# A fused sparse-attention and expert-attention kernel: the same 778 steps in another order, on other engines and buffers

## The chip, the cores and the metric

The kernel runs on one core of one Trainium2 chip. A core has five engines that run side by side, each with a queue of its own that it works off strictly in order: TensorE (PE, matmuls; its weight loads are shown apart as PEld), VectorE (DVE), ScalarE (ACT), GpSimd (POOL) and SyncE (SP, which here only issues transfers). POOL issues transfers too. PE writes to PSUM, a memory of 8 banks; DVE and ACT read it, POOL does not in this kernel. The metric is the time of one launch in microseconds (us), the median of several runs.

## What is computed

Two parts follow one another. The first is attention with 4 batches, 8 heads, 768 positions and 64 channels, in which a position sees its 31 nearest neighbours and 24 block summaries. The second sends the result x (4 x 768 x 512) through 4 causal attention experts, of which each position takes the best 2, weighted by a gate.

```python
k_sum = k.reshape(B, H, nb, 32, D).max(axis=3)
v_sum = v.reshape(B, H, nb, 32, D).mean(axis=3)
scores_l = scale * q @ k.T          # only where |i - j| < 16
scores_s = scale * q @ k_sum.T + log(32)
a = softmax(concat(scores_l, scores_s))
x = a @ concat(v, v_sum)            # heads side by side: (B, S, 512)
...
logits = x @ w_gate                 # top 2 of 4 experts, softmax over the two
for e in range(4):
    q, k, v = x @ wq[e], x @ wk[e], x @ wv[e]
    ye = causal_softmax(scale * q @ k.T) @ v @ wo[e]
    out += gate_weight[e] * ye
```

## The kernel before

**Tiling.** Stage 1 works on a pair of heads at a time (c = 0 to 3 in each batch b), stage 2 on a batch. The steps have names of a few letters followed by b, then c or another index. In stage 1:

- `dk`, `dq` (L285) load k and q through POOL's queue. In batch 0 the heads of pairs 2 and 3 come as one load (`dk010`, `dq010`), those of pair 1 and of pair 0 as one each (`dk001`, `dq001`, `dk000`, `dq000`). `dv` (L303 to L305) loads v through SP's queue into the tile vb, and `hc` (L181, shown as vb<-vb) copies the edge rows inside vb.
- `tk` and `tq` (L393) turn k and q on PE; `kw` and `cq` evict them from PSUM; `rk` (L410) takes the block maximum and `ksc` (kw<-ks) spreads it.
- `bs` (L322) sums blocks of v on PE, `be` (vs<-ps) evicts the sums and `ds` (vb<-vs) copies them into vb; for batches 2 and 3 POOL adds the blocks itself (`tr`, L367 and L370) and `ds` reads vu.
- `sc` (L435 and L441) are the scores, `ex` (L449) the exponential, `av` (L459) the product with v, `rc` and `xm` (L470, L474) the division, `tx` (L486) the turn of x, and `hi`, `lo` (L503) split x into two halves of half precision.

In stage 2: `vp` (L558, L561) makes v of all experts and the gate's logits, `v2` evicts the former, and `lg`, `ga`, `gx`, `gb`, `gc` (L568 to L607) turn the latter into gate weights. For two pairs of experts (cc = 0, 1), `pp` (L623) makes q and k, `pc` evicts them, `sp` (L647) are the scores in six units, `es` (L655) the exponential, `dm` (L660) the causal mask on POOL, `aw` (L671) the product with v, `r2` and `wv` (L691 to L698) the division and the gate weight, `tw` (L710) and `ct` turn the result; then `op` (L730) projects it, `oc` evicts it and `od` (L741) stores it. In the last batch the end is cut in two: `aw3?0` and `aw3?1` feed the cut of rows 0 to 511, `aw3?2` that of rows 512 to 767.

The weights of stage 2 come through POOL's queue: `dwq`, `dwk` (L516), `dwv` (L522, tile wvg) and `dwo` (L527). Small constants are set up once: `id16`, `id32`, `ke`, `mt`, `sel` on POOL, and clears (`vz`, `vone`, `kz`, `kwz`, `vtz`) on DVE or POOL. A few steps have a filler ahead of them (three matmuls on zeros, L169) that runs if the table gives it to PE and is left out if the table says N.

**What sets the order.** Nothing is scheduled at run time. `make_plan` lists 778 steps, each with the engines that may run it; `TABLE` is a list of entries `number,engine,slots`. `emit` goes through the table from front to back and writes each step's instructions to that engine's queue, with the buffer slots that the entry names. So the table's order, read for one engine, is that engine's queue, and a step waits for what it reads and for the last user of the slot that it writes. Some evictions and copies may run on two or three engines:

```python
R.step(f"hc{b}{c}", {"G": 1.65, "A": 1.45, "V": 0.9}, [vr[b, c]], [vb[b, c]], edge)
R.step(f"kw{b}{c}", {"V": 1.35, "A": 1.13}, [kp, kwpad], [kw], kwc)
```

The letters are V for DVE, A for ACT, G for POOL, S for SP and P for PE; the numbers beside them are not used in `emit`.

Of the kernel before, what the change touches and what calls it, by code (L numbers as in the profile page):

```python
# [58 lines left out]
101,P,3 102,A, 74,N,4 75,P,4 330,P,2.2.2 28,V, 76,A, 15,V, 80,P,0 81,P,1.1 97,N,4 45,N,3 79,A, 46,P,0 260,S,5 139,G,
333,V, 249,S,0 334,V, 33,N,6 82,P, 19,N,7 34,P,0 35,V, 332,A, 98,P,5 99,A, 428,G,0 50,A, 20,P,1 313,P,6.0.0 316,V,  # L60
314,P,2.2 318,A, 83,V, 84,V, 248,G,1 49,A, 51,N,4 52,P,0 21,V, 131,N,2 85,N,0 86,P,0.0 331,P,7.1 53,A, 315,A, 87,A,
132,P,1.1 22,V, 335,V, 88,V, 54,N,4 55,P,1 338,P,6.4 133,V, 32,A, 142,G, 427,G,2 57,N,0 58,P,1.2 36,V, 56,A, 59,P,
60,V, 261,G, 105,P,4.0.0 61,V, 103,N, 104,P, 134,V, 500,P,0.1.2 336,P,2.2 339,A, 141,G, 106,V, 337,A, 263,G, 107,V,
# [814 lines left out]
```

## Time and profile before

| | us |
|---|---|
| median of 3 runs (189.62, 191.22, 195.1) | 191.22 |
| the profiled execution: its time | 190.61 |
| the profiled execution: span from its first to its last instruction | 188.7 |
| PE busy in the span | 157.0 |
| chain that ended last: share of PE, DVE, ACT, DMA | 44%, 21%, 14%, 9% |
| packets of all DMA queues | 23.54 MB |

The profile gives the span of one execution, in which each instruction has a start and a length. What lies outside the span is 190.61 - 188.7 = 1.9 us. Of the rows that follow below, those of a timeline read: start, length, engine, line, operation, output tile <- input tiles, and in brackets how long the engine had been idle before and what released it. Those of a group read: busy time, mean length in ns, idle time before. Those of windows read: the stretch, its length, and the busy time of PE, PEld, DVE, ACT and POOL in it with the instructions in brackets, then the granted PE clock as a share of full speed, the DMA share, and GB/s.

### The profile page before, as it was taken

Reading aid. Unit: us, or ns where it says so; the run is one execution under the profiler, and the core shown is the slowest. Engines: PE = TensorE matmul, PEld = TensorE weight load, DVE = VectorE, ACT = ScalarE, POOL = GpSimd, SP = SyncE. Lnnn points to the kernel's source line nnn. Section 1 sums busy time; section 2 is a strip of 40 time slices with the busy share of each in tenths; the row PEclk is TensorE's granted clock in tenths of the full one; section 3 lists DMA queues with packets and bytes.
Section 4 is the critical chain, followed back from the end, with each engine's and each line's share of the span. In section 5 each row is a group of like instructions: output and inputs, shape, how many; then the busy total and the mean of one; then the engine's idle time right before and its main releaser. Section 6 shows DMA issues by size and latency. Waiting matters only on the chain.

```text
span 188.7 us, 7092 instructions
## 1 busy us (share of the span) xinstructions
PE 157.0 (83%) x3074; PEld 113.9 (60%) x3074; DVE 130.5 (69%) x253; ACT 121.2 (64%) x153; POOL 98.9 (52%) x155
## 2 busy tenths in 40 slices
PE   7419879598888997978899999897799998999670
PEld 2216668486666675865665688764575876547420
DVE  6794667899546789967629888696685684655740
ACT  2053376683568677868887886649688885697140
POOL 7868304983038269639847779129994141053000
PEclk9965589969999999999999999999999999999879
DMA  4999999999950006799969305498910530005325
GB/s 70 199 195 196 177 162 152 158 167 196 196 133 1 3 3 85 150 193 170 115 135 165 115 8 75 119 246 140 192 49 3 212 126 5 0 25 201 115 111 222
DMA packets 44207, 23.54 MB, mean 125 GB/s; under 512 B 33168, under 2 KB 39568, under 8 KB 44176
## 3 DMA queue, kind: packets, MB, share of 16 engines
q1 hardware_dynamic: 31136, 15.74, 40.6%
q0 software_dynamic: 13040, 7.34, 29.1%
q8 instruction: 24, 0.39, 0.9%
q14 instruction: 7, 0.06, 0.1%
HBM read 24.13 MB, written 6.29 MB: 161 GB/s over the span
## 4 chain that ended last, share of the span: by engine, by line
PE 44%; DVE 21%; ACT 14%; DMA 9%; issue 6%; POOL 3%; ACTq 1%; DVEq 0%; POOLq 0%
PE ps L623 9%; PE ps L459 8%; DMA wvg<-in_moe_wv_dram 5%; ACT a L655 5%; DMA qn<-in_q_dram 4%; PE ps L730 4%; PE ps L647 4%; PE ps L558 4%; ACT kw L179 3%; DVE vb L181 3%; DVE ks L410 3%; DVE x L474 3%; DVE lo L503 3%; PE ps L393 3%; PE ps L671 2%
## 5 line engine op out<-in xcount | busy, mean ns | idle before, releaser
L655 ACT ACTIVATE a<-ps 128x1024 f16<-128x1024 f32 (+1 forms) x48 | 42.1, 919 | 7.7 <-PE ps L647 6.0
L660 POOL TENSOR_SCALAR_AFFINE_SELECT a<-a 128x256 f16<-128x256 f16 x48 | 19.2, 418 | 39.0 <-ACT a L655 38.4
L449 ACT ACTIVATE aT<-ps 120x768 f32<-120x768 f32 x32 | 25.4, 814 | 14.1 <-PE ps L441 13.3
L459 PE MATMUL ps<-vb,aT 120*64 120x65 f32 x768 | 28.7, 231 | 1.6 <-issue 1.0
L459 PEld LDWEIGHTS ps<-vb,aT 120*64 120x64 f32 x768 | 26.1, 145 | 4.8 <-issue 3.3
L623 PE MATMUL ps<-hi,wqk 128*128 128x384 f16 x128 | 23.0, 327 | 1.4 <-DVE lo L503 0.5
L181 POOL COPY vb<-vb 32x1536 f32<-32x1536 f32 x11 | 16.4, 1501 | 8.0 <-DMA vb<-in_v_dram 7.6
L179 ACT COPY kw<-ps 128x1152 f16<-128x1152 f16 x13 | 14.4, 1118 | 9.5 <-DVE ks L410 9.0
L410 DVE TENSOR_REDUCE ks<-ps 128x24 f16<-128x768 f16 x16 | 15.2, 951 | 4.8 <-ACT kw L179 2.6
L647 PE MATMUL ps<-qk,qk 64*128 64x512 f16 (+3 forms) x128 | 15.7, 308 | 2.8 <-ACT a L655 1.5
L367 POOL TENSOR_TENSOR vt<-vt 120x1024 f32<-120x1024 f32 (+1 forms) x8 | 14.7, 1841 | 5.1 <-DMA vt<-in_v_dram 4.9
L623 PEld LDWEIGHTS <-wqk 128*128 128x128 f16 x128 | 12.0, 97 | 8.8 <-issue 1.1
L503 DVE TENSOR_TENSOR lo<-ps,hi 128x768 f16<-128x768 f32 x16 | 15.3, 954 | 1.7 <-ACT hi L179 1.5
L474 DVE TENSOR_TENSOR x<-ps,rec 128x768 f32<-128x768 f32 x16 | 15.3, 958 | 0.6
L558 PE MATMUL ps<-wvg,hi 128*128 128x264 f16 x96 | 14.0, 275 | 0.9 <-DVE ob L181 0.5
L671 PE MATMUL ps<-v,a 128*128 128x65 f16 x336 | 13.1, 194 | 1.9 <-DVE wav L698 0.8
L441 PE MATMUL ps<-qT,kw 64*128 64x64 f16 x384 | 12.1, 197 | 3.0 <-DVE qT L181 1.3
L730 PE MATMUL ps<-wo,wT 128*128 128x512 f16 x48 | 13.3, 406 | 1.5 <-ACT wT L179 1.1
L441 PEld LDWEIGHTS <-kw 64*128 64x128 f16 x384 | 10.7, 99 | 6.1 <-issue 2.9
L671 PEld LDWEIGHTS <-a 128*128 128x128 f16 x336 | 11.5, 97 | 4.3 <-issue 3.3
L179 ACT CAST qk<-ps 128x768 f16<-128x768 f32 x11 | 8.9, 806 | 6.5 <-PE ps L623 5.7
L322 PE MATMUL ps<-vb,sel 64*32 64x128 f32 x208 | 9.4, 307 | 4.3 <-POOL sel L266 3.5
(101 smaller groups left out, 289.3 us busy)
## 6 DMA issues: line engine op xcount, KB each, us to landing
vb<-in_v_dram SPq DMA_DIRECT2D x32, 176.0 KB
out_dram<-ob SPq DMA_DIRECT2D x11, 512.0 KB
vt<-in_v_dram SPq DMA_DIRECT2D x16, 192.0 KB
kn<-in_k_dram POOLq DMA_DIRECT2D x7, 384.0 KB, 6.5
qn<-in_q_dram POOLq DMA_DIRECT2D x7, 384.0 KB, 8.9
out_dram<-ob SPq DMA_DIRECT2D x2, 256.0 KB
vb<-in_v_dram SPq DMA_DIRECT2D x16, 24.0 KB
kn<-in_k_dram POOLq DMA_DIRECT2D x2, 192.0 KB, 8.6
```

The source lines that it names most:

```text
L179: nc.scalar.copy(dst, src)
L181: en(e).tensor_copy(dst, src)
L441: nc.tensor.matmul(s[:, hp, 64 * t:64 * t + 64], T["kw"][kw.slot][r, tt, :], T["qT"][qT.slot][r].rearrange("d (s p) -> d s p", s=8)[:, :, ...
L449: nc.scalar.activation(T["aT"][aT.slot][0:KR], pbank(sc, 2)[0:KR, :, 0:384], AF.Exp, scale=SCALE)
L459: nc.tensor.matmul(pbank(av, 2)[o:o + 64, u, 65 * (2 * (t // 2) + hp):65 * (2 * (t // 2) + hp) + 65], a[0:KR, hp, 64 * t:64 * t + 64], T[" ...
L474: nc.vector.tensor_tensor(T["x32"][x32.slot].rearrange("p (u t w) -> p u t w", u=2, w=64), avv()[:, :, :, 0:64], T["rec"][rec.slot].to_bro ...
L503: nc.vector.tensor_tensor(turned(T["lo"][lo.slot]), xpv(), turned(T["hi"][hi.slot]), AL.subtract)
L558: nc.tensor.matmul(p[:, i, 0:264], hi_(ch)[:, cols], T["wvg"][:, ch, :], start=(ch == 0), stop=False, skip_group_check=True)
L623: nc.tensor.matmul(pbank(pp, 2)[:, u, 0:384], T["wqk"][:, cc, ch, j, :], hi_(ch)[:, 384 * u:384 * u + 384], start=(ch == 0), stop=(ch == N ...
L647: nc.tensor.matmul(pbank(sp, 2)[:, ep, c0:c0 + w], T["qk"][qk[1].slot][r, 128 * tj:128 * tj + 128], T["qk"][qk[0].slot][r, n0:n0 + w], sta ...
L655: nc.scalar.activation(a2v(u), pbank(sp, 2)[:, :, 0:ln], AF.Exp, scale=SCALE / (XS * XS))
L671: nc.tensor.matmul(pbank(av, 2)[:, ep, 65 * ti:65 * ti + 65], a2v(u)[:, ep, o:o + 128], T["v2"][v2.slot][:, tj, 2 * cc + ep, :], start=(tj ...
```

## The change

Only `TABLE` changes; the steps, what they compute and the number of buffers stay.

```diff
 TABLE = """
-29,G,0 30,G,0 0,V, 112,P,0 66,P,1 91,P,2 114,P,3 5,G, 3,G,1 4,G,1 1,G, 123,N,4 89,N,6 16,V, 6,G, 258,G,2 11,V,
...
+29,G,0 135,S, 11,V, 0,V, 112,N,0 3,G,1 43,N,1 89,N,2 7,V, 66,N,3 9,V, 5,G, 8,V, 6,G, 14,G, 12,G, 90,P,0.0 93,V,
...
```

Every step is in both tables once. What differs is the order on each queue, the slots, and the engine of 83 steps. Of these:

| step | before | after |
|---|---|---|
| `kw` (16) | 3 DVE, 13 ACT | 7 DVE, 9 ACT |
| `cq` (16) | 8 DVE, 8 ACT | 12 DVE, 4 ACT |
| `ds` (16, two copies each) | 8 DVE, 8 POOL | 2 DVE, 12 POOL, 2 ACT |
| `hc` (16) | 1 DVE, 4 ACT, 11 POOL | 4 DVE, 6 ACT, 6 POOL |
| `hi` (16) | 8 DVE, 8 ACT | 6 DVE, 10 ACT |
| `pc` (16) | 5 DVE, 11 ACT | 7 DVE, 9 ACT |
| `ksc` (16) | 6 DVE, 6 ACT, 4 POOL | 4 DVE, 5 ACT, 7 POOL |
| `vone`, `vtz`, `v2o` (clears) | DVE | POOL |
| `cg` (gate weights to half) | POOL | DVE |
| fillers that run (3 matmuls each) | 6 | 2 |

**The start on POOL.** Before, POOL's queue begins with the loads of k and q for pairs 2 and 3 (kn_78, qn_74), and goes on to those of the other pairs (kn_79 and qn_75):

```order
L285 DMA kn_78<-in_k_dram 96x4x512
L285 DMA qn_74<-in_q_dram 96x4x512
L201 MEMSET id_64 128x128
L202 ISA
L202 AFFINE_SELECT id_64<-id_64 128x128
L285 DMA kn_79<-in_k_dram 96x2x512
L285 DMA qn_75<-in_q_dram 96x2x512
L285 DMA kn_79<-in_k_dram 96x2x512
```

After, the queue begins with the loads of kn_78 and kn_79 and the constants id16, ke, id32, vone and sel, of which the last row of sel stands first here; then come the q load, the masks, and a copy (`ksc03`) that reads a block maximum made by DVE, and the other loads behind that:

```order
L266 AFFINE_SELECT sel<-sel 64x4
L285 DMA qn_74<-in_q_dram 96x4x512
L224 MEMSET mt 128x128
L227 AFFINE_SELECT mt<-mt 64x96
L228 AFFINE_SELECT mt<-mt 64x96
L227 AFFINE_SELECT mt<-mt 64x96
L228 AFFINE_SELECT mt<-mt 64x96
L181 COPY kw_85<-ks_82 128x12x24
L285 DMA qn_75<-in_q_dram 96x2x512
L285 DMA kn_79<-in_k_dram 96x2x512
L285 DMA qn_75<-in_q_dram 96x2x512
L272 MEMSET vt_101 128x2112
```

The load of qn_74 moved from second place to behind 17 setup instructions, and those of pairs 1 and 0 to behind a wait for DVE; sel and vone moved ahead of all q loads.

**The end on DVE.** The gate weights of the last batch (gt_126) end with L607; what follows in DVE's queue before is the division of the last batch (cmb, wav) at once:

```order
L604 TENSOR_TENSOR ps<-gt_126,ps 128x24
L605 TENSOR_REDUCE gt_126<-ps 128x6
L606 RECIPROCAL gt_126<-gt_126 128x6
L607 TENSOR_TENSOR gt_126<-ps,gt_126 128x24
L691 RECIPROCAL ps<-ps 128x2x2
L693 TENSOR_TENSOR cmb_133<-ps,gt_126 128x2x2
L691 RECIPROCAL ps<-ps 128x2x2
L693 TENSOR_TENSOR cmb_132<-ps,gt_126 128x2x2
L698 TENSOR_TENSOR wav_135<-ps,cmb_133 128x2x2x64
L698 TENSOR_TENSOR wav_134<-ps,cmb_132 128x2x2x64
```

After, three evictions of the batch before stand between (wT, and ob of two outputs):

```order
L604 TENSOR_TENSOR ps<-gt_126,ps 128x24
L605 TENSOR_REDUCE gt_126<-ps 128x6
L606 RECIPROCAL gt_126<-gt_126 128x6
L607 TENSOR_TENSOR gt_126<-ps,gt_126 128x24
L181 COPY wT_137<-ps 128x2x6x64
L181 COPY ob_140<-ps 128x1024
L181 COPY ob_142<-ps 128x1024
L691 RECIPROCAL ps<-ps 128x2x4
L693 TENSOR_TENSOR cmb_132<-ps,gt_126 128x2x4
L698 TENSOR_TENSOR wav_135<-ps,cmb_132 128x2x4x64
```

The gate moved ahead of older work, and the larger cut (128x2x4) now comes before the smaller one (128x2x2).

**The end on ACT.** ACT evicts the last outputs (ob) and the last turned results (wT). Before:

```order
L179 CAST v_124<-ps 128x8x64
L593 ACTIVATE gt_126<-gt_126 128x24
L655 ACTIVATE a_131<-ps 128x256
L179 COPY ob_141<-ps 128x1024
L179 COPY wT_138<-ps 128x2x2x64
L179 COPY ob_140<-ps 128x512
L179 COPY ob_141<-ps 128x1024
L179 COPY ob_140<-ps 128x1024
```

After:

```order
L179 COPY ob_141<-ps 128x1024
L179 COPY wT_138<-ps 128x2x4x64
L655 ACTIVATE a_130<-ps 128x256
L179 COPY ob_140<-ps 128x1024
L179 COPY ob_142<-ps 128x1024
L179 COPY wT_138<-ps 128x2x2x64
L179 COPY ob_141<-ps 128x512
L179 COPY ob_140<-ps 128x512
```

The two outputs of 1024 columns now come ahead of the two of 512, and v and the gate's exponential have moved up out of this place. On PE the three `vp` of the last batch stand, before, behind 9 to 11 of its 12 `sp` and all its `pp`; after, behind 3 to 5 `sp` and ahead of the second pair's two `pp`.

More of the change, by code (lines that the diff above doesn't have):

```diff
@@ L59 @@
[L59 to L63, printed above, removed]
@@ L104 @@
-724,P,1.1.0 729,V, 762,V, 722,P, 730,V, 763,V, 755,P, 756,P, 758,V, 731,P,4.2 764,P,2.3 765,V, 596,S, 590,S, 759,V,
-723,P, 732,A, 772,P,2.0 773,A, 774,S, 725,V, 726,V, 760,P,6 727,P,4 761,V, 728,V, 775,P,3.2 776,V, 777,S, 766,P,0.1
-767,A, 768,S, 769,P,6.0 770,A, 771,S,
+29,G,0 135,S, 11,V, 0,V, 112,N,0 3,G,1 43,N,1 89,N,2 7,V, 66,N,3 9,V, 5,G, 8,V, 6,G, 14,G, 12,G, 90,P,0.0 93,V,
+113,P,1.1 39,P,4 116,A, 91,P,5 94,V, 13,G, 67,P,2.2 120,N,6 117,V, 70,V, 30,G,0 114,N,2 115,P,0 10,G, 25,N,0 71,V,
@@ new lines @@
+107,V, 21,V, 444,S,0 108,N,4 109,P,1.1 51,N,0 52,P,2 110,A, 333,V, 139,G, 136,G, 22,G, 140,G, 78,P,0 111,V, 18,V,
+57,N,2 28,A, 53,A, 292,N,4 293,P,1.2 297,V, 296,A, 445,G, 79,A, 80,N,0 81,P,0.2 58,P,1.0 82,P, 251,S,1 83,V, 84,V,
+446,G,0 59,P, 269,N,5 85,N,6 334,A, 338,P,0.1 60,V, 61,V, 314,P,4.0 318,V, 339,A, 62,N,2 63,P,2.2 142,V, 261,A,
+86,P,3.3 87,V, 264,N,4 88,V, 265,P,1 162,N,0 64,A, 65,V, 163,P,0 200,N,6 201,P,1 197,N,2 202,A, 266,V, 271,N,4
+164,V, 268,G, 207,N,6 249,S,2 270,P,2.1 274,V, 272,P,2 276,A, 198,P,2 143,N,0 144,P,0 16,G, 199,A, 219,N,2 220,P,0
@@ new lines @@
+472,P,0.2 473,A, 306,P,4.1.1 307,P, 432,G, 329,V, 308,V, 309,V, 288,N,6 232,N,0 233,P,0 234,A, 194,N,2 195,P,1
+196,V, 289,P,6.6 290,A, 310,P,4.7.7 311,A, 291,V, 429,S,5 430,A, 235,N,0 312,V, 236,P,0 237,V, 239,N,2 240,P,1
+612,S,2 389,P,6.2 500,P,4.1.0 390,V, 502,A, 610,S,4 484,P,5.2 488,V, 487,A, 503,V, 435,G,1 391,P,0.0 447,G, 437,G,
+491,P,6.0 392,V, 436,G, 449,P,5.2.2 452,V, 241,A, 501,P,4.0 402,P,0.0 451,V, 393,P,2 492,A, 347,P,6.1 394,A, 504,V,
+403,A, 353,P,2 354,V,5 350,P,0 355,V, 349,A, 505,A, 348,V, 352,A, 351,V, 356,V,1 597,G,2 357,A, 508,P,2.4 453,V,
@@ new lines @@
+611,G, 379,P,4 513,V, 374,A, 380,A, 370,P,6 461,V, 462,V, 623,G, 371,A, 398,G, 367,P,0 603,S,0 637,P,4.0 641,V,
+620,P,5.1 624,V, 463,P,2.2.2 368,A, 410,G, 395,G, 640,G, 644,P,6.0 645,A, 613,V, 627,P,4.5 628,A, 464,V, 465,V,
+401,G, 407,G, 413,P,0.0.0 514,P,6.3.3 625,P,4.3 412,P, 411,P, 515,A, 530,P,2.2 516,V, 604,G, 600,A, 531,A, 381,G,
+626,A, 414,V, 378,G, 605,G,1 375,G, 415,V, 532,P,6.0 372,G, 674,V, 678,P,2.4 607,G,0 533,V, 606,G, 238,S, 676,P,4.2
+601,S, 679,A, 642,P,0.1 677,A, 546,P,6.0 643,A, 630,P,2.1.0 654,P,4.1 658,V, 629,P, 631,V, 547,A, 534,P,0 535,A,
@@ new lines @@
+632,V, 416,P,4.2 417,V, 517,P,6.0 518,V,0 519,V, 523,P,2 525,V, 524,V, 537,P,4 538,A, 540,P,6 653,P,1.0.1 656,V,
+655,A, 520,P,2 522,A, 521,V, 526,V,0 559,P,4.1 366,G, 614,S,0 527,A, 528,V, 529,V, 369,G, 383,P,1.1.2 382,P, 541,A,
+560,A, 615,G, 616,G,0 539,G, 617,G, 384,P, 542,G, 549,P,0 550,A, 242,S, 657,G, 659,P,6.5 385,V, 386,V, 661,P,4.3
+660,A, 543,P,0 662,A, 387,P,2.3 388,V, 561,P,6.0 562,V, 618,A, 418,P,4.0 419,V, 544,A, 548,G, 421,P,2.1 422,A,
+420,S, 633,P,6.4.4 572,P,4.1 573,A, 563,P,0 564,A, 565,G, 634,V, 680,P,2.0.1 681,P, 575,P,4 566,P,0 635,V,
@@ new lines @@
+664,P,6.1.2 663,P, 576,A, 682,V, 683,V, 684,P,4.5.5 569,P,2 567,A, 568,G, 602,V, 646,P,0.0.0 647,P, 665,V, 666,V,
+685,A, 686,V, 424,P,6.0 648,V, 570,A, 649,V, 577,G, 571,G, 578,P,4 579,A, 425,V, 667,P,2.6.6 650,P,0.7.7 581,P,0.0.4
+574,G, 582,P, 580,G, 545,G, 583,P, 668,A, 669,V, 651,A, 733,P,6.2 536,G, 652,V, 735,P,2.0 736,A, 734,V, 551,G,
+554,P,1.1.0 552,P, 743,P,2.1 752,P,6 584,V, 585,V, 753,A, 426,S, 749,P,4 553,P, 687,P,6.1 555,V, 556,V, 750,A,
+688,V,0 744,A, 689,A, 690,P,4 692,A, 691,V, 751,G, 246,S, 557,P,2.0 737,P,6 423,S, 558,V, 746,P,4 747,A, 738,A,
@@ new lines @@
+693,P,2 694,V, 695,A, 696,V,1 697,A, 702,P,4.1 703,A, 740,P,6 700,P,2.0 741,A, 742,G, 586,P,4.1 739,G, 698,V, 699,V,
+701,A, 710,P,6.0 711,A, 712,G, 713,P,0 587,V, 748,G, 714,A, 715,G, 594,P,2.0 595,V, 707,P,6 708,A, 596,S, 745,G,
+588,P,4.2 589,V, 590,S, 709,G, 704,P,0 705,A, 706,G, 754,G, 716,P,2 717,A, 756,P,1.0.6 755,P, 591,P,4.1 718,G,
+592,A, 593,S, 722,P,0.1.0 758,V, 759,V, 723,P, 760,P,2.2 757,P, 761,A, 719,P,4 725,V, 726,V, 727,P,2.3 728,V,
+769,P,2.0 720,A, 770,A, 766,P,4.2 762,V, 771,S, 763,V, 721,G, 724,P, 764,P,2 729,V, 730,V, 767,A, 768,S, 731,P,6
@@ L107 @@
+732,V, 765,A, 775,P,0.1 776,A, 777,S, 772,P,1.0 773,A, 774,S,
 """
```

64 lines of the change are left out of this document (20 added, 44 removed).

## The prediction

> **What bounds the kernel now.** I read the busy line and the slices first, then windows of the stages, then the timeline of the two ends.
>
> ```profile
> span 188.7 us, 7092 instructions
> PE 157.0 (83%) x3074; PEld 113.9 (60%) x3074; DVE 130.5 (69%) x253; ACT 121.2 (64%) x153; POOL 98.9 (52%) x155
> ...
> DMA  4999999999950006799969305498910530005325
> ...
> 0.00:48.00 48.00, 34.40 (x725) 26.25 (x726) 36.62 (x70) 23.70 (x28) 28.34 (x54) 0.82 1.26 168
> 48.00:154.50 106.50, 96.67 (x2029) 72.20 (x2029) 76.95 (x140) 79.69 (x104) 65.45 (x88) 1.00 0.60 115
> 154.50:172.00 17.50, 16.77 (x202) 10.36 (x199) 10.05 (x16) 12.99 (x17) 4.68 (x12) 1.00 0.15 55
> 172.00:189.00 17.00, 9.21 (x126) 5.12 (x124) 6.92 (x27) 4.78 (x8) 0.41 (x1) 0.89 0.35 131
> ```
>
> PE is the busiest engine, but its waits lie unevenly. In the first window, up to the first `pp`, it is busy 34.40 of 48 us at a clock of 0.82, while the transfers run full (eleven slices of 4.7 us, to 52). In the middle it works 96.67 of 106.5 us at full clock: 9.8 us of waits. From 154.5 to 172 it hardly waits. In the last 17 us it is busy 9.21. So an order can win at most 10 us in the middle, and the rest at the two ends. I take each stretch by itself.
>
> **The start: -2.3 us.** The last `lo` of batch 0 on DVE releases the first `pp`:
>
> ```profile
> 47.99 2.76 PE L623 MATMUL ps<-hi,wqk 128*128 128x384 f16 x16 [0.51 <-DVE lo L503]
> ...
> 34.00:48.00 14.00, 10.31 (x255) 8.68 (x250) 13.50 (x22) 9.08 (x12) 9.49 (x13) 0.88 1.39 179
> ...
> L181 DVE COPY kw<-ps 128x1152 f16<-128x1152 f16 x3 | 3.9, 1333 | 0.0
> L181 DVE COPY qT<-ps 128x768 f16<-128x768 f16 x8 | 4.4, 552 | 0.2
> L181 DVE COPY vb<-vs 24x768 f32<-24x768 f32 x10 | 7.6, 797 | 0.1
> L181 DVE COPY vb<-vb 32x1536 f32<-32x1536 f32 x1 | 1.2, 1189 | 0.0
> L181 DVE COPY kw<-ks 128x288 f16<-128x288 f16 x6 | 1.7, 279 | 0.1
> L272 DVE MEMSET vt<- 128x2112 f32 x1 | 1.8, 1818 | 0.5 <-issue 0.5
> ...
> 174.68 0.18 DVE L607 TENSOR_TENSOR gt<-ps,gt 128x24 f32<-128x24 f32 x1
> ```
>
> DVE is full from 34 to 48 (13.50 of 14), so DVE's queue sets this end. Up to its last `lo` of batch 0 the new queue holds less: 3 `ds` of two copies, 6 x 0.80 = 4.8; 4 `ksc`, 1.1; `vtz`, 1.8. It holds more: 2 `kw`, 2.7; 2 `cq`, 1.1; 2 `hc`, 2.4; `cg`, four small operations like the one at 174.68, 0.7. That is 7.7 less and 6.9 more. The five small clears of `vone` leave too, at most 0.18 each; I count 0.6. If DVE idles as long as before, the first `pp` comes 1.4 us earlier. What is moved to POOL and ACT here lies under their own idle time (28.34 and 23.70 busy of 48).
>
> How long DVE idles is set by the loads and by PE's early speed:
>
> ```profile
> 3.79 0.15 PEld L169 LDWEIGHTS <-zz 128*128 128x128 f16 x1 [0.28 <-issue]
> 4.21 1.39 PEld L169 LDWEIGHTS <-zz 128*128 128x128 f16 x7 [0.27 <-issue]
> ...
> 7.72 0.90 PE L393 MATMUL ps<-ke,kn 100*64 100x100 f16 x32 [1.62 <-DMA kn<-in_k_dram]
> ...
> 14.51 1.91 PE L322 MATMUL ps<-vb,sel 64*32 64x128 f32 x26 [3.47 <-POOL sel L266]
> ...
> 17.11 0.88 PE L393 MATMUL ps<-ke,kn 100*64 100x100 f16 x16
> ...
> 22.89 2.40 PE L459 MATMUL ps<-vb,aT 120*64 120x65 f32 x48
> ...
> 1.35 0.82 POOL L285 DMA_DIRECT2D kn<-in_k_dram  x1 [0.85 <-POOLq L862]
> 2.17 0.68 POOL L285 DMA_DIRECT2D qn<-in_q_dram  x1
> ...
> 4.02 0.63 POOL L285 DMA_DIRECT2D qn<-in_q_dram  x1
> ...
> 11.15 0.22 POOL L224 MEMSET mt<- 128x128 f16 x1
> ...
> 12.41 0.26 POOL L228 TENSOR_SCALAR_AFFINE_SELECT mt<-mt 64x96 f16<-64x96 f16 x1
> ...
> DMA to landing us min/median/max: 4.8/8.9/13.9
> ```
>
> `bs03` waits 3.47 us for `sel` on POOL; `sel` now stands early, and this wait goes. In its place q is late. The five instructions of the masks run from 11.15 to 12.67, 0.30 each; 17 setup instructions are 5.2 by that. The q load, issued at 2.17 before, is issued at 1.35 + 0.82 + 0.65 + 5.2 = 8.0 after. The last row is the landing of the q loads, from the view of the tile qn: 12.8 at the least, 16.9 at the median. I take 13.5, near the least, because only two k loads stand ahead of it. From there PE has work without a gap: `tq03` and `tq02` 1.8, `bs01` and `bs03` 3.8, `sc030` 0.8, `tq01` 0.9, three `sc` 2.5, `tq00` and `tk00` 1.8, `av031` 1.2, `bs02` 1.9, `av030` 1.2, all at the speed of the rows at 14.51, 17.11 and 22.89 (an `sc` is an estimate, two of the shorter turns' pace): the end is at 29.4. Before, the same `av` ended at 25.3, without four of these steps (4.5). PE stands level.
>
> That was half speed. The spacing of the fillers' weight loads falls from 0.42 (3.79 to 4.21) to 0.20 (7 in 1.39): PE sped up after 3 us of unbroken work. Then it idled, and 16 turns at 17.11 cost what 32 did at 7.72. If the unbroken run from 13.5 lifts the speed likewise, `bs03` and `bs02` take half, 1.9 less, and DVE, which waits for both, gains up to 3.3 in all; if PE stays slow as it did before from 14.5 to 24, 1.4. I take the middle, **-2.3**. Of the six fillers four go; that costs at most two `tk` at half speed, 0.9, which lies under the wait for q. Ends: -4, and with late q (below) +4.6.
>
> [...]
>
> **The middle: +0.9 us.** From the first `pp` of batch 0 to that of batch 3 PE's work is the same but for steps that cross the edges: in come `tk12`, `tk23`, `sc130`, `sc121` and `aw210`, out go `bs12` and `tk11`. A `tk` is 0.45 (7.72), a `bs` 0.95 (half of 14.51), an `aw` of 12 matmuls 0.5 (175.30, below), and an `sc` 12.1 / 32 = 0.4 by the first row here:
>
> ```profile
> L441 PE MATMUL ps<-qT,kw 64*128 64x64 f16 x384 | 12.1, 197 | 3.0 <-DVE qT L181 1.3 <-ACT kw L179 0.9 <-issue 0.8
> ...
> 120.00:140.00 20.00, 16.74 (x320) 12.23 (x320) 16.04 (x33) 13.44 (x19) 13.55 (x15) 1.00 0.79 172
> 140.00:160.00 20.00, 19.47 (x382) 13.82 (x374) 12.69 (x18) 15.49 (x21) 7.20 (x14) 1.00 0.23 82
> ```
>
> The waits, 9.8, I leave. DVE's work there grows by some 5 us on 76.95, ACT's falls by some 7 on 79.69 (counted from the queues with the rows' lengths); both keep idle time. The waits' bounds are the worst and best window: 3.26 of 20 over 106.5 us would be 17.4 (+7.6), 0.53 of 20 would be 2.8 (-7.0). Two loads come later: `dwv` behind `ds00`, and `dwo` behind the last mask of batch 0's first expert pair. Their first users, `vp00` and `op00`, stand some 5 us and more of PE's work behind; I count 0.
>
> **The end: -2.8 us.** Before, `vp` ends late, and the gate on DVE (to 174.68) holds up the division:
>
> ```profile
> 175.30 0.53 PE L671 MATMUL ps<-v,a 128*128 128x65 f16 x12 [0.55 <-DVE cmb L693]
> 176.67 0.77 PE L671 MATMUL ps<-v,a 128*128 128x65 f16 x20 [0.84 <-DVE wav L698]
> 177.37 0.29 PE L710 MATMUL ps<-id,wav 64*128 64x64 f16 x8
> 177.60 0.41 PE L671 MATMUL ps<-v,a 128*128 128x65 f16 x8
> 177.81 0.28 DVE L181 COPY wT<-ps 128x256 f16<-128x256 f16 x1
> 179.00 0.40 PE L710 MATMUL ps<-id,wav 64*128 64x64 f16 x8
> 179.11 0.58 ACT L179 COPY ob<-ps 128x512 f32<-128x512 f32 x1 [1.09 <-PE ps L730]
> 179.72 5.04 SPq L741 DMA_DIRECT2D out_dram<-ob  x4
> 180.12 3.08 PE L730 MATMUL ps<-wo,wT 128*128 128x512 f16 x10
> ```
>
> After, `vp` stands ahead of two `pp` and seven `sp`, the gate hides under them, and the waits of 0.55 and 0.84 go: -1.4. Before, the last `aw` ends at 178.01 and the span 10.7 later. After, behind the last `aw` stand: division and gate weight 0.8 (estimated, five small operations), the turn 0.29, its eviction 0.28, two outputs of two matmuls (4 x 0.31 = 1.2 by 180.12), an eviction 0.58, six hand-overs of some 0.05, and the store; the last issue on SP ends at 184.76, the span 3.9 later. Sum 7.4: -3.3. Against that, more of PE's work stands ahead of the last `aw`: before, 0.8 of turns and 3.1 of outputs came behind it, after, 0.3 and 1.2; 2.4 more, less 0.5 of `aw210`: +1.9. Together **-2.8**. Ends: -4.8, if the smaller store lands in half the time, and -0.3, if ACT sets this end: its work from the last batch's first `pc` on is 2.5 us more than before.
>
> **Sum.** 188.7 - 2.3 + 0.9 - 2.8 = 184.5 of span; with 1.9 outside, 186.4, against 190.61 for the same execution. The median, 191.22, is 0.6 above that one, so I predict **187.0 us**.
>
> **Rivals.** Late q: `dq001`, `dk000` and `dq000` stand behind `ksc03`, which waits for `rk03` on DVE until about 11.5 (an estimate: three operations behind the first `tk`). Before, `dq001` was issued at 4.02; after, at 12. PE needs `tq01` at 19.9 in the walk above. At the longest landing, 13.9, it comes at 25.9: 6.0 late, and the speed-up is gone. The start is then -1.4 + 6.0 = +4.6, the span 191.4, the time **193.9**: slower than before. It decides from a landing of 11.2 us on. For it: the transfers run full. Against it: fewer loads stand in POOL's queue then.
>
> Given back: an order of three engines that each have 70 to 90% of work may wait more in the middle. At +4.2, some half of the way to the worst window, the time is 191.2, **no change**.
>
> Tighter: half of the way to the best window, -3.5, gives **183.5**.
>
> Slow end: ACT sets the end, and the start gains DVE's plain sum alone: -1.4 + 0.9 - 0.3, the time 190.4.
>
> **How the numbers follow.** A difference under 2% is about what a measurement of this kernel can't tell from none; the bounds are 187.4 and 195.0. The forecast has 0.42, with its own range 184.5 to 189.0, and 0.27 of it under 187.4; tighter 0.20, all faster; given back 0.16, of which 0.03 beyond 195.0; slow end 0.07, within; late q 0.15, of which 0.09 beyond 195.0, if the middle waits more too. Faster 0.47, same 0.41, slower 0.12. The range takes in all but the outer parts of tighter and late q: 182.0 to 194.5.
>
> **What would show it.** The first L623 at about 45.7 (the start is right from 44 to 46.6); the first L393 on qn at 13 to 14; PE's clock at 1.00 by 20 if the unbroken run lifts it; no wait of PE for `sel`; no wait of L671 for cmb or wav in the last 20 us; the last L671 some 7 us before the end. The forecast is wrong if the second group of L393 on qn comes after 22, if PE waits over 13 us between the two `pp`, or if ACT works without a gap in the last 15 us.

## The result and the profile after

| | before | after |
|---|---|---|
| median, us (5 runs each) | 191.22 | 188.52 |
| lowest to highest | 189.46 to 195.1 | 187.13 to 188.94 |
| the profiled execution: its time, its span | 190.61, 188.7 | 187.13, 185.4 |

The ratio is 0.9843, 95% interval [0.9801, 0.9885]: about 1.6% faster, which the bound of 2% calls the same. A second measurement (six runs, below as e13_after) gave medians of 189.67 and, before, 192.07, and a ratio of 0.9723 [0.9646, 0.98]. The ratios leave out the runs that lie over 1.5% above a kernel's fastest, and these kernels' runs scatter by about 3%, so that a ratio rests on a kernel's quicker runs (on two of the six in the second measurement) and can lie lower than the ratio of the medians.

These are lines of the page of the kernel after:

```profile
span 185.4 us, 7057 instructions
...
PE 152.6 (82%) x3062; PEld 112.2 (61%) x3062; DVE 132.5 (71%) x248; ACT 118.7 (64%) x148; POOL 100.0 (54%) x165
...
PEclk9996696996999969999999999999999999999996
DMA  4999999999599928669395689207200306300745
...
q8 instruction: 24, 0.39, 0.9%
```

The transfers run full up to the tenth slice, to some 46 us (before to the eleventh, 52 us), and again behind it from 51 to 65 us. PE is still the busiest engine. The windows that the prediction used, of the kernel after (columns as before):

```profile
0.00:48.00 48.00, 32.12 (x716) 25.85 (x718) 35.27 (x61) 20.86 (x25) 31.45 (x58) 0.86 1.31 165
48.00:154.50 106.50, 96.56 (x2042) 71.67 (x2035) 82.40 (x149) 78.62 (x98) 63.76 (x96) 0.98 0.56 102
...
34.00:48.00 14.00, 10.07 (x264) 8.86 (x257) 9.72 (x19) 8.53 (x11) 9.52 (x10) 0.88 1.54 163
```

In the first 48 us DVE is busy 35.27 us (36.62 before). From 34 to 48 us, where it had 0.5 us of idle time before, it is busy 9.72 of 14. Cut at the first `pp` (L623) of batch 0 and that of batch 3, the two executions compare thus:

| stretch, us | before | after | difference | forecast |
|---|---|---|---|---|
| start, to the first L623 of batch 0 | 47.99 | 48.32 | +0.3 | -2.3 |
| middle, to the first L623 of batch 3 | 106.5 | 106.3 | -0.2 | +0.9 |
| end, to the end of the span | 34.2 | 30.8 | -3.4 | -2.8 |

So in these two executions the whole gain lies in the end, and the start gave nothing. PE's timeline in the start of the kernel after, with its waits:

```profile
14.20 0.87 PE L393 MATMUL ps<-id,qn 96*64 96x96 f16 x32 [2.05 <-DMA qn<-in_q_dram]
14.99 3.49 PE L322 MATMUL ps<-vb,sel 64*32 64x128 f32 x52
...
19.17 0.85 PE L393 MATMUL ps<-id,qn 96*64 96x96 f16 x16
...
22.00 0.53 PE L393 MATMUL ps<-id,qn 96*64 96x96 f16 x16
...
26.51 0.55 PE L393 MATMUL ps<-ke,kn 100*64 100x100 f16 x16 [0.99 <-DMA kn<-in_k_dram]
26.89 0.51 PE L393 MATMUL ps<-id,qn 96*64 96x96 f16 x15
28.95 0.24 PE L393 MATMUL ps<-id,qn 96*64 96x96 f16 x1 [1.55 <-issue]
...
35.86 0.34 PE L435 MATMUL ps<-pi,mt 64*128 64x384 f16 x2 [0.92 <-issue]
...
37.80 0.55 PE L393 MATMUL ps<-ke,kn 100*64 100x100 f16 x16 [1.09 <-DVE lo L503]
...
41.78 2.31 PE L459 MATMUL ps<-vb,aT 120*64 120x65 f32 x48 [1.84 <-ACT aT L449]
...
48.32 1.93 PE L623 MATMUL ps<-hi,wqk 128*128 128x384 f16 x9
```

PE waits 6.4 us between 25.5 and 42 us: for a k load, for `lo` on DVE, for an exponential on ACT, and 2.47 us for "issue", which is nothing that the profile shows. (The kernel before has 4.8 us of waits from 25 us to its first L623.) The stall at 28.95 is odd: fifteen turns of q run, and the sixteenth, with the same operands at hand, comes 1.55 us late. DVE in turn waits for PE; this is its queue:

```profile
42.91 0.23 DVE L470 RECIPROCAL rec<-ps 128x12 f32<-128x12 f32 x1 [3.04 <-PE ps L459]
```

The first L623 has no wait in the kernel after: PE comes to it straight from other work, while before it waited 0.51 us for DVE's `lo`. PE's own queue reaches this point last, though only just: of the last two `hi` that these matmuls read, that on ACT ends at 48.22 us, 0.1 us ahead of the first, and that on DVE at 48.74, while they run.

The end of the kernel after, by its timeline:

```profile
166.41 0.18 DVE L607 TENSOR_TENSOR gt<-ps,gt 128x24 f32<-128x24 f32 x1
...
171.15 11.35 SPq L741 DMA_DIRECT2D out_dram<-ob  x7
...
177.97 0.83 PE L671 MATMUL ps<-v,a 128*128 128x65 f16 x22
...
180.37 1.04 PE L730 MATMUL ps<-wo,wT 128*128 128x512 f16 x4 [0.39 <-DVE wT L181]
181.05 1.07 ACT L179 COPY ob<-ps 128x512 f32<-128x512 f32 x2 [1.54 <-PE ps L730]
```

The gate is done at 166.41 instead of 174.7, and no `aw` waits for it. The last `aw` ends at 178.80, 6.6 us before the end of the span; before, it ended 10.7 us ahead of it.

### The profile page after: what moved, and what is told of

Same layout as the page of the kernel before. It is cut to its first block, busy times and chain, and to the rows that moved or that the text cites. A ratio compares the mean times of both kernels' runs of the same rounds, so it can differ in the third digit from the quotient of the medians.

```text
span 185.4 us, 7057 instructions
## 1 busy us (share of the span) xinstructions
PE 152.6 (82%) x3062; PEld 112.2 (61%) x3062; DVE 132.5 (71%) x248; ACT 118.7 (64%) x148; POOL 100.0 (54%) x165
## 4 chain that ended last, share of the span: by engine, by line
PE 48%; DVE 23%; ACT 10%; issue 6%; DMA 5%; POOL 5%; ACTq 0%; DVEq 0%; POOLq 0%
PE ps L459 11%; PE ps L623 8%; PE ps L730 6%; DMA kn<-in_k_dram 5%; PE ps L558 5%; DVE ks L410 5%; PE ps L647 4%; ACT kw L179 4%; PE ps L393 3%; PE ps L671 3%; PE ps L486 2%; PE ps L435 2%; DVE lo L503 2%; ACT a L655 2%; ACT aT L449 2%
## 5 line engine op out<-in xcount | busy, mean ns | idle before, releaser
L623 PE MATMUL ps<-hi,wqk 128*128 128x384 f16 x128 | 23.7, 333 | 0.5 <-DVE lo L503 0.4
L179 ACT COPY kw<-ps 128x1152 f16<-128x1152 f16 x9 | 10.1, 1121 | 14.2 <-PE ps L393 8.2
L623 PEld LDWEIGHTS <-wqk 128*128 128x128 f16 x128 | 12.0, 99 | 9.1 <-issue 2.1
L393 PE MATMUL ps<-ke,kn 100*64 100x100 f16 x256 | 9.2, 221 | 9.4 <-POOL sel L265 7.4
L393 PEld LDWEIGHTS <-kn 100*64 100x64 f16 x256 | 7.3, 118 | 12.4 <-issue 10.2
L181 POOL COPY vb<-vs 24x768 f32<-24x768 f32 x10 | 8.0, 825 | 11.9 <-DVE vs L340 11.8
L181 POOL COPY vb<-vu 24x768 f32<-24x768 f32 x14 | 11.5, 823 | 3.3 <-PE ps L459 2.6
L435 PE MATMUL ps<-pi,mt 64*128 64x384 f16 x64 | 12.0, 364 | 1.2 <-issue 0.9
L671 PE MATMUL ps<-v,a 128*128 128x65 f16 x336 | 12.4, 193 | 0.5 <-DVE ps L568 0.5
```

The costliest lines, as they stand in the source:

```text
L181: en(e).tensor_copy(dst, src)
L393: nc.tensor.transpose(dst[64 * hp:64 * hp + 64, n * s:n * s + n], src[:, hh + hp, 64 * s:64 * s + 64], mov)
L623: nc.tensor.matmul(pbank(pp, 2)[:, u, 0:384], T["wqk"][:, cc, ch, j, :], hi_(ch)[:, 384 * u:384 * u + 384], start=(ch == 0), stop=(ch == N ...
L671: nc.tensor.matmul(pbank(av, 2)[:, ep, 65 * ti:65 * ti + 65], a2v(u)[:, ep, o:o + 128], T["v2"][v2.slot][:, tj, 2 * cc + ep, :], start=(tj ...
```

## The experiments

Two questions were open: what took the gain of the start, and which part of the new end is worth what. For the start there were three theories. A: the order on ACT, since an exponential stands behind `kw11`. B: the k load of `tk13`, which comes late. C, formed after the first runs: the "issue" stalls, as a limit of their own. In the first four kernels the line numbers are one lower (L392 there is L393 here). The diffs show entries of `TABLE`.

### e1_ex and e2_dk: the two waits of the start

In e1_ex the exponential `ex011` (79) stands ahead of `kw11` (296) on ACT; in e2_dk the loads `dq110` (259) and `dk110` (258) stand ahead of the clear `vtz` (15) on POOL.

```diff
-296,A, 445,G, 79,A,
+79,A, 296,A, 445,G,
```

```diff
+258,G,2 259,G,2
 15,G,
...
-259,G,2
...
-258,G,2
```

> The changed kernel with one step moved on ACT: the exponential ex011 stands ahead of the eviction kw11 instead of behind it. Theory A (in the changed order DVE idles longer before the last lo of batch 0, because ACT holds ex011 behind kw11, which waits for DVE): the two av at 41.78 start at about 40.0, DVE's idle 3.0 before L470 at 42.91 shrinks to about 1.2, the first L623 comes at 46.5 instead of 48.32, the time falls by about 1.8 us to some 186.7. Rival B (late k of batch 1 and the half clock behind it set the start): the av move up, but the first L623 moves by less than 0.5 and the time stays at 188 to 188.6.

> The changed kernel with POOL's queue in another order at one place: dk110, dq110, then the clear vtz, instead of vtz, dq110, dk110. Theory B (the late k of batch 1 holds up PE, which idles from 25.5 to 29 and falls to half speed): dk110 is issued at 13.9 instead of 16.3 and lands 2 us or more earlier, tk13 starts when av030 ends (25.5), the clock stays at 1.00 from 26 to 33, and the first L623 comes 1 to 2 us earlier, time 186.5 to 187.5. Rival A: the gap closes, but the first L623 moves by less than 0.5, since ACT's queue sets it.

Measured: e1_ex 190.9 us median, ratio to before 0.9846 [0.9759, 0.9934], which is what the kernel after has; first L623 at 48.45. e2_dk 190.12 us median over 185.33 to 193.65, no ratio: inconclusive in time; first L623 at 51.01 in its profiled run, which took 191.79 us. Rows of PE's timeline of e1_ex:

```profile
35.11 0.34 PE L434 MATMUL ps<-pi,mt 64*128 64x384 f16 x2 [2.03 <-issue]
43.15 0.57 PE L458 MATMUL ps<-vb,aT 120*64 120x65 f32 x13 [2.39 <-issue]
```

and of e2_dk:

```profile
26.78 0.53 PE L392 MATMUL ps<-id,qn 96*64 96x96 f16 x15 [0.64 <-DMA qn<-in_q_dram]
30.19 0.24 PE L392 MATMUL ps<-id,qn 96*64 96x96 f16 x1 [2.89 <-issue]
```

The wait that each edit was aimed at went: in e1_ex the 1.84 us for the exponential, in e2_dk the 0.99 us for the k load. Each time stalls stand in its place: 2.03 us instead of 0.92 and a new one of 2.39 in e1_ex, 2.89 instead of 1.55 in e2_dk. The stalls sit before the same matmuls in all these kernels. In e1_ex PE passes them at 28.17 and 35.11, against 28.95 and 35.86 in the kernel after; in e2_dk at 30.19. A and B are both true as waits, and in neither run did the first L623 come earlier. But it isn't shown that the edits removed the waits. These are rows of e3_gate_late, whose start has the order of the kernel after:

```profile
27.25 0.53 PE L392 MATMUL ps<-ke,kn 100*64 100x100 f16 x16
...
30.20 0.20 PE L392 MATMUL ps<-id,qn 96*64 96x96 f16 x1 [2.09 <-issue]
...
43.15 2.57 PE L458 MATMUL ps<-vb,aT 120*64 120x65 f32 x48 [0.48 <-ACT aT L448]
```

Here, and in e13_after as well, the wait for the k load is gone without either edit (PE comes to these turns 0.7 and 0.3 us later than in the kernel after), and that for the exponential is 0.48 and 0.30 us, with stalls of 3.32 and 5.31 us. Waits and stalls of this start trade places from one execution to the next.

### e7_shift and e10_fetch: what the stalls are

Counting PE's matmuls up to a stall shows the pattern. These are rows of windows of the kernel after, each up to one of its two stalls:

```profile
0.00:28.94 28.94, 17.00 (x347) 12.58 (x348) 22.45 (x39) 10.26 (x12) 19.60 (x45) 0.88 1.19 163
0.00:35.85 35.85, 23.00 (x474) 17.58 (x474) 26.97 (x48) 13.41 (x17) 21.95 (x49) 0.86 1.25 165
```

The stalls come after 347 and 474 matmuls, 127 apart; e1_ex has a third after 601, 127 on. The kernel before has its stalls of 0.48, 1.03 and 0.50 us after 475, 1363 and 1491, which are 7 and 8 times 127 from the first, less a matmul or so. With their weight loads, 127 matmuls are 254 instructions. The row of queue q8 above has 24 packets with 0.39 MB, some 16 KB each; PE's 3062 matmuls and 3062 weight loads over 24 are 255 (the row doesn't say which engine's program a packet holds). Theory C is therefore that PE's program comes by DMA in pieces of some 255 instructions, and that a piece is late while the transfers run full.

e7_shift tests the place: the first four fillers are switched on, which puts 12 matmuls ahead of everything.

```diff
-112,N,0
+112,P,0
...
-43,N,1 89,N,2
+43,P,1 89,P,2
...
-66,N,3
+66,P,3
```

> The kernel after with its first four fillers switched on (4 of 3 matmuls, while PE waits for sel until 7.4 us): 12 matmuls more ahead of everything. Theory C (pieces of 127 matmuls): the first stall comes again after 347 matmuls and the second after 474, so 12 matmuls earlier in the program: the first not before the 16th of the sixteen matmuls of tq13 (L393 on qn) but before the 4th. Rival D (the stall belongs to that place of the program): it stays before the last matmul of tq13, now after 359. Rival E: no fillers, slow clock; with fillers the clock is full earlier and the start is 1 us or more shorter. By C alone the first L623 is where it was, 48.3 to 49.9, median 187.5 to 190.

The stall of e7_shift, in PE's timeline, and the count up to it:

```profile
29.66 0.72 PE L393 MATMUL ps<-id,qn 96*64 96x96 f16 x13 [2.07 <-issue]
```

```profile
0.00:29.65 29.65, 18.86 (x347) 12.82 (x348) 21.95 (x39) 10.25 (x12) 20.00 (x45) 0.88 1.21 159
```

It comes again after 347 matmuls, now before the fourth of the sixteen turns: 12 earlier in the program, as C expects, and not at its old place in the program. There is none after 474, where PE has a wait for DVE (0.96 us) at that very place, and one of 1.13 us after 601. The fillers brought no earlier start: the q load came late (a wait of 4.52 us at 15.13), the first L623 at 51.35, the median 190.71 us, both over the 48.3 to 49.9 and 187.5 to 190 expected by C alone.

e10_fetch measures the stall by itself: PE runs 762 small matmuls, each with its weight load, then 1651 more, while loads of v, k and q of the kernel's shapes start behind the first 762.

```python
stream(0, 762)
...
stream(1, 1651)
```

> The stall by itself; nothing of the reference is computed. PE runs 762 small matmuls (six pieces of 127, each matmul with its weight load) with no transfer under way, then 1651 more, while SP and POOL start some 4.5 MB of v, k and q loads of the kernel's shapes. Theory C: 'issue' stalls of PE come 127 matmuls apart; while the transfers run full each is longer than in the quiet stretch by 1 us or more, and behind the last load they fall back. Rival (pieces come in time whatever the transfers do): no difference between the stretches.

PE's timeline of e10_fetch; the first v load is issued at 21.68:

```profile
1.19 19.04 PE L115 MATMUL ps<-zz 128*32 128x32 f16 x735 [1.19 <-DVE zz L111]
20.61 3.35 PE L115 MATMUL ps<-zz 128*32 128x32 f16 x128 [0.38 <-issue]
24.34 3.35 PE L115 MATMUL ps<-zz 128*32 128x32 f16 x128 [0.38 <-issue]
31.35 3.58 PE L115 MATMUL ps<-zz 128*32 128x32 f16 x128 [3.67 <-issue]
37.82 3.52 PE L115 MATMUL ps<-zz 128*32 128x32 f16 x128 [2.90 <-issue]
45.39 3.57 PE L115 MATMUL ps<-zz 128*32 128x32 f16 x128 [4.05 <-issue]
50.22 13.71 PE L115 MATMUL ps<-zz 128*32 128x32 f16 x512 [1.25 <-issue]
64.58 3.35 PE L115 MATMUL ps<-zz 128*32 128x32 f16 x128 [0.65 <-issue]
```

and two of its windows (PE, PEld, DVE, POOL, clock, DMA share, GB/s):

```profile
22.00:52.00 30.00, 17.76 (x658) 17.34 (x655) 0.82 (x1) 4.08 (x6) 0.70 1.02 154
52.00:80.00 28.00, 25.39 (x974) 24.81 (x970) 0.00 (x0) 0.00 (x0) 0.96 0.02 4
```

By the spacing of the gaps a piece is 128 matmuls with their weight loads, 256 instructions. With no transfers under way, the first 735 matmuls, over five pieces, run without a gap that the timeline sets apart, and so do the four pieces from 50.22 us; where there is a gap between two pieces, it is 0.38 to 0.65 us. While the loads run, the gaps are 3.67, 2.90 and 4.05 us, and the pieces come 7.0, 6.5 and 7.6 us apart, though a piece itself takes some 3.5 us; a last gap of 1.25 us stands where the loads have just ended. C holds for these stalls: at a DMA share of 1.02 (22 to 52 us) a piece begins every 6.5 to 7.6 us, though the inputs of its matmuls, zeros on the chip, are ready. In the kernel after the two stalls are 6.9 us apart, which is that pace.

### e6_hold, e9_hold_ex and e11_hold_before: other loads in the start

In e6_hold the v loads of batch 1 take the buffers of batch 0 as these come free, rather than two empty ones; later loads swap buffers accordingly. In the table `dv12` (260) stands behind `av030` and `dv13` (262) behind `av021`; `dv11` (251) and `dv10` (249) stay and change their buffer. e9_hold_ex adds the edit of e1_ex. e11_hold_before holds the same loads back in the kernel before: there `dv13` goes behind `av030`, `dv12` behind `av011`, `dv10` behind `av001`, each into the buffer of that chunk, and `dv11` into that of chunk 2. The diff is that of e6_hold.

```diff
-260,S,4
...
 127,P,
+260,S,1
...
-262,S,5
...
 105,P,
+262,S,2
...
-251,S,1
+251,S,0
...
-249,S,2
+249,S,3
```

> The kernel after, in which four v loads of the second batch take the buffers of the first batch as these come free (dv12 behind the last av of chunk 3, some 26 us, instead of 15.7; dv13 behind that of chunk 2, some 33; dv11 and dv10 behind 41) instead of two empty ones, so that the transfers are not full from 22 to 40 us. Theory C, PE's program comes by DMA in pieces of some 127 matmuls with their weight loads (the row of queue q8: 24 packets, 0.39 MB; 3062 matmuls and 3062 weight loads over 24 is 255) and a piece is late while the transfers are full: the 'issue' stalls after 347 and 474 matmuls, 1.55 and 0.92 us after the change, shrink to under 0.8 together, and the first L623 comes at 46 to 47 instead of 48.3; median 186 to 188.5. Rival D, the start is set by DVE's and ACT's queues and the stalls only fill time in which PE would wait anyway: first L623 at 48 to 49, median 188 to 190. If bs12 waits for the late loads, it does so just before the first L623, and both are late by what it waits.

> The loads held back as in e6_hold, and on ACT the exponentials ex011 ahead of kw11. By theory C the run with ex011 alone lost its gain to stalls of 1.31, 2.03 and 2.39 us after 347, 474 and 601 matmuls; with the loads held back these shrink to under 1.2 together and the earlier av counts: first L623 at 44.5 to 46, median 184.5 to 187.5. By rival D (queues of DVE and ACT set the start) no earlier than e6_hold, within 0.5 us.

> The kernel before with the same holding back of the second batch's v loads as in e6_hold. Before's start had one stall of 0.48 us and no wait for a k load, so by theory C there is little to win: first L623 within 1 us of before's 48.0 to 49.5, ratio 0.99 to 1.01. If the loads' order is what the start hangs on in any order of the engines, it gains as after did: first L623 at 47 or earlier, ratio under 0.985.

| | median, us | before on that chip | ratio, interval | first L623 | issue stalls ahead of it |
|---|---|---|---|---|---|
| e6_hold | 188.47 | 192.32 | 0.9691 [0.9615, 0.9766] | 47.09 | 0.71, 1.03 |
| e9_hold_ex | 185.94 | 192.32 | 0.9665 [0.9561, 0.9769] | 46.45 | 1.20, 1.76 |
| e11_hold_before | 193.81 | 192.07 | 1.0104 [1.0048, 1.016] | 48.73 | 0.75 |

The kernel before does not gain from it, 1% slower; C expected 0.99 to 1.01. Whether the kernel after gains is not settled: its own ratio is 0.9843 in one measurement and 0.9723 in the other. The sizes missed: the stalls of e6_hold did not fall under 0.8 us together, and those of e9_hold_ex not under 1.2; the first L623, at 47.09 and 46.45, came just behind the expected 46 to 47 and 44.5 to 46. The edit did not empty the queues: over the first 48 us the DMA share is 1.27 in e6_hold, against 1.31. Other loads ran in the place of the held ones. In the trace of e6_hold PE no longer waits for the k load of `tk13`, and its wait for the exponential is 0.39 us instead of 1.84; but e3_gate_late has nearly the same (none and 0.48) without this edit. And the profiled run of e6_hold is the fastest of its ten, 183.73 us against a median of 188.47: of the 3.4 us that its span is shorter than that of the kernel after, 1.2 lie in the start and 2.2 in the middle (104.1 us against 106.3). What the start would be with no stall at all was not shown.

e9_hold_ex says something else about the start. Rows of its PE timeline, and one of its windows:

```profile
15.89 3.62 PE L322 MATMUL ps<-vb,sel 64*32 64x128 f32 x52
...
20.19 0.85 PE L393 MATMUL ps<-id,qn 96*64 96x96 f16 x16
...
28.92 0.20 PE L393 MATMUL ps<-id,qn 96*64 96x96 f16 x1 [1.20 <-issue]
```

```profile
14.00:22.00 8.00, 7.53 (x134) 5.93 (x136) 4.83 (x13) 2.81 (x4) 6.80 (x10) 1.00 1.35 178
```

Here the record grants PE the full clock from 14 to 22 us, where the kernel after has 0.57. Yet the block sums and the turns take as long as there (3.49 and 0.85 us), and PE passes its 347th matmul at the same time, 28.92 against 28.95.

### e3_gate_late, e4_cut_order and e8_end: the end

e3_gate_late is the kernel after with the last batch's `vp`, `v2` and gate (13 steps) moved behind the score unit `es301`. e4_cut_order is the kernel after with rows 512 to 767 cut first and the 512 KB stores last, as before. e8_end is the kernel before up to the first `pp` of batch 3, and from there the order of the kernel after. The first diff shows the first and the last moved step of e3_gate_late (`vp30`, 687, and `gc3`, 699; 717 is `es301`), the second the table's last entries in e4_cut_order.

```diff
-687,P,6.1
...
-699,V,
...
 717,A,
+687,P,6.1
...
+699,V,
```

```diff
-732,V, 765,A, 775,P,0.1 776,A, 777,S, 772,P,1.0 773,A, 774,S,
...
+728,V, 769,P,2.0 770,A, 771,S, 766,P,4.2 767,A, 768,S,
```

> The changed kernel with the last batch's vp, v2, lg, ga, gx, gb and gc moved back behind its last large sp (as before), all else of the changed order kept. If the end's gain comes from hiding the gate (the forecast's term of 1.4), the wait for cmb or wav comes back, the span from the first L623 of batch 3 to the end grows from 30.8 by 1.4 to 2.5, time 190 to 191. Rival (the gain comes from the order of the two cuts and the smaller last store): it grows by less than 0.7, time 188.5 to 189.2.

> The changed kernel with the order of the two cuts of the last batch turned back: rows 512 to 767 first, rows 0 to 511 and their two stores of 512 KB last. By the forecast's terms (3.3 less behind the last aw, 1.9 more ahead of it) the end grows by some 1.4 to 2, time 190 to 190.5. Rival (only the hidden gate counts): it grows by less than 0.7.

> The kernel before up to the first pp of the last batch, and from there the order of after (gate early, large cut first). If the end's gain is a matter of the end's order alone, the stretch from the first L623 of batch 3 to the end is 30.8 as in after (34.2 before), and the median 187.3 to 188.8 (before less 2.4 to 3.9). If it hangs on what after did earlier, it is 32.5 or more and the median over 189.

| | gate of the last batch | cut first | first L623 of batch 3 to the end | median, ratio to before |
|---|---|---|---|---|
| before | late | small | 34.2 | |
| e3_gate_late | late | large | 38.8 | 197.52, 1.0236 [1.0114, 1.0359] |
| e4_cut_order | early | small | 34.0 | 192.16, 1.0018 [0.9967, 1.0069] |
| after | early | large | 30.8 | 188.52, 0.9843 [0.9801, 0.9885] |
| e8_end | early | large | 31.8 | 190.02, 0.992 [0.9872, 0.9968] |

The two parts don't add up. In the orders tried, the early gate with the old cut gains 0.2 us, the new cut with a late gate loses 4.6, and both together gain 3.4. Against the kernel after, e3_gate_late is 8.0 us longer and e4_cut_order 3.2; 1.4 to 2.5 and 1.4 to 2 were expected. In e3_gate_late PE stops and starts:

```profile
165.09 2.72 PE L622 MATMUL ps<-hi,wqk 128*128 128x384 f16 x8 [1.11 <-ACT a L654]
...
180.44 0.77 PE L670 MATMUL ps<-v,a 128*128 128x65 f16 x20 [1.55 <-DVE gt L606]
```

The `vp` group no longer fills PE while ACT works on the exponentials, the same eight L623 that take 1.46 us in the kernel after take 2.72, and the second group of `aw` of the batch waits for the gate. So part of the 8.0 us is PE's slower pace and not waiting: in the same run eight more L623, at 168.24, take 1.47 us. A late gate in another place was not tried. e8_end shows that most of the end can be carried over: 2.4 us shorter than before in its profiled run. At 31.8 us it lies between the 30.8 that its expectation had for an end that stands by itself and the 32.5 of its rival. Its whole gain, 0.8% by the ratio (190.02 us against 192.32 by the medians), is less than the 1.2 to 2% that was expected of it.

### e12_hold_ex and e13_after: the best version beside the kernel after

e12_hold_ex is e9_hold_ex once more, e13_after the kernel after once more, with more rounds and on one chip; neither has another edit.

> e9_hold_ex once more, with more rounds and beside the kernel after on the same chip. If its gain over after holds: median 1.5 to 3.5 us below after's, first L623 at 46 to 47.5. If it was the draw of a chip: within 1 us of after's.

> The kernel after once more, for its start: theory C expects issue stalls after 347, 474 and perhaps 601 matmuls, 1.5 to 4 us together, and the first L623 at 48.3 to 50; median 187.5 to 190.

Measured on that chip: before 192.07, after 189.67, hold_ex 186.58 us. The ratios to before are 0.9723 [0.9646, 0.98] and 0.9687 [0.9624, 0.975]. By medians hold_ex is 3.1 us faster than after; by the ratios, whose intervals overlap, 0.4%. Over the three measurements of the held loads the ratio is 0.967 to 0.969 each time, over the two of the kernel after 0.984 and 0.972. So hold_ex beats the kernel before by about 3%, and probably the kernel after by 0.4 to 1.6%, which these runs don't settle. e13_after had stalls of 1.25, 2.03 and 2.03 us after 347, 474 and 601 matmuls, 5.3 together, somewhat over the 1.5 to 4 expected, and its first L623 at 50.13. In e12_hold_ex the first L623 came at 47.24 but had to wait for `hi` after one matmul, and only at 49.24 went on: the expected 46 to 47.5 holds by the letter alone.

## Why the prediction came out as it did

The forecast was 187.0 us, the median 188.52, inside the range. That the sum was nearly right is luck in part: a term that failed by 2.6 us and two that came out better than forecast, by 1.1 and 0.6, partly cancelled. The profiled execution took 187.13 us where 186.4 was forecast; the 0.6 us by which the median was to lie above it were 1.4.

**The start failed, by 2.6 us.** The load of q came nearly as forecast: the first L393 on qn at 14.20 instead of 13.5, and the second group at 19.17, far from the 22 that would have meant the rival of the late q. The step that failed is DVE's plain sum, by which "the first `pp` comes 1.4 us earlier", together with its condition, "If DVE idles as long as before". The sum was to go up to the last `lo` of batch 0. That one ends at 49.07 us before and at 50.59 after, and these are the windows up to there, before and after:

```profile
0.00:49.07 49.07, 35.47 (x731) 26.92 (x732) 37.58 (x71) 24.49 (x28) 28.34 (x54) 0.83 1.26 169
0.00:50.59 50.59, 34.58 (x733) 27.16 (x734) 37.83 (x63) 21.08 (x25) 31.96 (x59) 0.87 1.25 158
```

DVE's work grew by 0.25 us where 1.4 less was forecast. (In the first 48 us alone it fell by 1.35, but there the kernel after still has its last two `lo` ahead of it.) Two terms were mis-sized: the six copies of `ds` that left had taken 3.8 us and not 4.8, since in the start one takes some 0.63 us against the mean of 0.80 over the whole kernel; and `cg` takes 1.4 us, not 0.7. DVE's idle time up to there grew from 11.5 to 12.8 us, where the forecast had 0.9 less. And the first `pp` did not hang on the last `lo`: before, the `lo` that released it was the third of the four, from 46.99 to 47.94, and after, the first `pp` starts 2.3 us ahead of the end of the last one (1.1 before). The three together give the +0.3 measured.

DVE's longest wait in this start, the 3.04 us at 42.91, is for PE. The forecast took it that PE "has work without a gap" once q is there, and that the unbroken run would lift its pace and with it DVE's supply. PE did get the unbroken run to 25.5 us, but the pace fell from some 15 us on and rose again only at some 22 us (32 turns 0.87 us at 14.20, sixteen 0.85 at 19.17, sixteen 0.53 at 22.00), so that `bs03` was slow and only `bs02` ran at the better pace. And then PE stalled, by theory C for the arrival of its own program: 2.47 us ahead of the first L623, where the kernel before had 0.48. In the starts of e3_gate_late and e4_cut_order, which have the same order there, it was 3.32 and 2.34 us, with the first L623 at 49.89 and 48.77. What these stalls cost is not shown: no run took them away, the start of e8_end, with the order of the kernel before, has 0.24 us of them and its first L623 at 49.51 all the same, and that of e9_hold_ex has 2.96 us and is at 46.45. Besides, 1.84 us of wait stand at the exponential behind `kw11`, which moved to ACT and was counted as lying "under their own idle time".

How firm such numbers are can be read from the other traces in which a stretch has the same order:

| stretch, us | order of before | order of after |
|---|---|---|
| start | 48.0; 49.5 (e8_end) | 48.3; 49.9 (e3_gate_late), 48.8 (e4_cut_order), 50.1 (e13_after) |
| middle | 106.5; 108.7 (e8_end) | 106.3; 106.8 (e3_gate_late), 107.2 (e4_cut_order), 107.1 (e13_after) |
| end | 34.2; 34.4 (e11_hold_before) | 30.8; 30.8 in e2_dk, e6_hold, e7_shift, e9_hold_ex, e12_hold_ex and e13_after, 31.2 in e1_ex |

The gain of the end stands clear of the scatter. A start or a middle of one and the same order differs by up to 2 us between executions, so that the +0.3 and the -0.2 can't be told from nothing; but none of the four starts comes near the 45.7 forecast.

Why the same limit cost the kernel before so little is not shown by an experiment. Its piece up to 475 matmuls fell into a dip of the transfers, by its windows:

```profile
30.00:34.00 4.00, 4.00 (x127) 3.40 (x121) 2.37 (x8) 2.62 (x3) 2.94 (x4) 1.00 1.06 125
```

while the kernel after has, in the window of its second stall:

```profile
34.00:38.00 4.00, 2.00 (x59) 1.49 (x52) 3.50 (x8) 3.20 (x5) 2.17 (x3) 1.00 1.79 187
```

**The middle: +0.9 forecast, -0.2 measured.** PE's waits stayed (9.8 us before, 9.9 after), as forecast; PE's work there didn't grow (96.67 to 96.56). DVE's grew by 5.4, as the "some 5" had it; ACT's fell by 1.1 and not by 7, on which nothing hung. The terms of PE's work listed there add up to 0.8, not 0.9.

**The end: -2.8 forecast, -3.4 measured.** The mechanism was right on each point: the gate is hidden, no `aw` waits for it, the last `aw` ends 6.6 us before the end (some 7 forecast). The mis-sized term is what follows the last `aw`, 7.4 us forecast, 6.6 measured: the last store ends 2.9 us after SP's last issue (171.15 + 11.35 = 182.50), and not 3.9 as with the larger store before. From the first L623 of batch 3 to the end of the last `aw` it is 24.2 us against 23.6 before, +0.7, where the forecast had +1.9 and -1.4, +0.5. What the forecast did not see is that the two parts can't be priced one by one: of the -1.4 for the gate and the -3.3 behind the last `aw`, neither was to be had alone in e3_gate_late and e4_cut_order.

**The rivals.** Late q fell with the landing. Given back in the middle, at +4.2, and the tighter middle, at -3.5, both fell with the middle's -0.2. Slow end fell: ACT is busy 7.20 of the last 14 us. Of the signs that the prediction named, three did not come: the clock was not at 1.00 by 20 (0.57 from 14 to 22), the first L623 did not come at 44 to 46.6, and the profile puts PE's first wait, 7.36 us ahead of its first matmul, down to `sel` on POOL. The block sums themselves, at 14.99, no longer wait for it, which is what was meant.
